# Two rows of wo per partition, loaded in 16 loads of 8 partitions on 8 of the 16 DMA engines

## Chip, cores, metric

One core of a Trainium2 chip. The metric is device time in microseconds (us), median over runs. A program on one core shows no second state here: all timed runs of both kernels count as fast.

## The reference, cut

```python
def _A_ref(x, k_cache, v_cache, wq, wo):        # B=2, Sq=1, D=512, H=32, Sk=8192, Dh=128, bf16
    q = (x @ wq).reshape(B, Sq, H, Dh).transpose(0, 2, 1, 3)
    scores = einsum("bhqd,bhkd->bhqk", q, k_cache) * (Dh ** -0.5)
    o = einsum("bhqk,bhkd->bhqd", softmax(scores), v_cache)
    return o.transpose(0, 2, 1, 3).reshape(B, Sq, H * Dh) @ wo
...
return x + _A_ref(layernorm(x), k_cache, v_cache, wq, wo) + relu_mlp(layernorm(x), w1, w2)
```

One token attends to 8192 cached positions. The two caches are 268 MB, so the kernel is a stream from memory with a short end: the last values, then `o @ wo`.

## The kernel before: the parts concerned

SP, the engine whose sequencer issues the loads, puts every large load on one queue (q1, 280.50 of the 280.66 MB). The matrix wo (4 MB, 32 rows of 1 KB on each of 128 partitions) comes last, in five chunks of rows, each with its own semaphore. PE, the matrix engine, waits for one chunk at a time and multiplies four times per row.

```python
wo_v = A_wo.rearrange("(p j) n -> p j n", j=WJ)          # WJ = 32 rows a partition
cuts = (0, 14, 21, 27, 30, WJ)
...
# SP
for i in range(2):                                        # the last V block, in two halves
    sl = slice(i * SLOT // 2, (i + 1) * SLOT // 2)
    sp.dma_start(vs[(NP - 1) % R][:, sl], V_all[(NP - 1) * P:NP * P, sl]).then_inc(dH[i], 16)
for c in range(NC):
    sl = slice(cuts[c], cuts[c + 1])
    sp.dma_start(wo_sb[:, sl, :], wo_v[:, sl, :]).then_inc(dW[c], 16)
sp.wait_ge(sE, 1)
sp.dma_start(out.rearrange("b s (c p) -> (b s c) p", p=P), osb[:]).then_inc(dO, 16)
...
# PE
for c in range(NC):
    pe.wait_ge(dW[c], 16)
    for j in range(cuts[c], cuts[c + 1]):
        for k in range(KT):                               # KT = 4
            t = pe.matmul(fin[:, k, :], lhsT=wo_sb[:, j, k * P:(k + 1) * P], rhs=OX[:, j, :],
                          start=False, stop=(j == WJ - 1 and k == KT - 1))
```

Of the kernel before, what the change touches and what calls it, by code (L numbers as in the profile page):

```python
# [19 lines left out]
def kernel(  # L20
# [13 lines left out]
    P = 128  # L34
# [3 lines left out]

    Bsz, Sq, D = A_x.shape
    _, H, Sk, Dh = A_k_cache.shape  # L40
    Dff = B_w1.shape[1]
    assert Dh == P and D % P == 0 and Dff % P == 0 and Sk % HP == 0
# [5 lines left out]
    WJ = H * Dh // P  # L48
# [18 lines left out]
    def sem(name):  # L67
        return tc.alloc_semaphore(name)
# [8 lines left out]
    wo_sb = w_sb[:, 0:WJ * D].rearrange("p (j n) -> p j n", j=WJ)  # L77
# [52 lines left out]
    dW = [sem(f"dWo{i}") for i in range(5)]  # L130
# [9 lines left out]
    K_all = A_k_cache.rearrange("b h (m kk) d -> (b h m) (kk d)", kk=KB)  # L140
    V_all = A_v_cache.rearrange("b h (m kk) d -> (b h m) (kk d)", kk=KB)
    wo_v = A_wo.rearrange("(p j) n -> p j n", j=WJ)
    cuts = (0, 14, 21, 27, 30, WJ)
    NC = len(cuts) - 1
    qp = ot[0][0:QG * Bsz, :]
    tpq = tp[1][:].rearrange("p g k -> p (g k)")[:, 0:N].rearrange(
# [10 lines left out]
    def load_k(t):  # L157
        nc.sync.dma_start(ks[t % R][:], K_all[t * P:(t + 1) * P, :]).then_inc(dK[t % R], 16)

    def load_v(t):  # L160
        nc.sync.dma_start(vs[t % R][:], V_all[t * P:(t + 1) * P, :]).then_inc(dV[t % R], 16)

    nc.sync.dma_start(vs[1][:], A_wq.rearrange("(p kt) n -> p (kt n)", kt=KT)).then_inc(dV[1], 16)  # L163
    nc.scalar.dma_start(xsb[:], A_x.flatten_outer_dims()).then_inc(dX, 16)
# [2 lines left out]
    @(lambda f: f(nc.sync))  # L167
    def _(sp):
        sp.dma_start(w1_sb, B_w1.rearrange("(p kt) f -> p kt f", kt=KT)).then_inc(dW1, 16)  # L169
        sp.dma_start(w2_sb, B_w2.rearrange("(p j) n -> p j n", j=FT)).then_inc(dW2, 16)  # L170
        load_k(0)
        load_k(1)
        load_v(0)
        for t in range(NP - 2):
            sp.wait_ge(pT[NG - 1], t + 1)
            load_k(t + R)
            sp.wait_ge(sW, t + 1)
            load_v(t + 1)
        sp.wait_ge(sW, NP - 1)
        for i in range(2):  # L180
            sl = slice(i * SLOT // 2, (i + 1) * SLOT // 2)
            sp.dma_start(  # L182
                vs[(NP - 1) % R][:, sl], V_all[(NP - 1) * P:NP * P, sl]
            ).then_inc(dH[i], 16)
        for c in range(NC):
            sl = slice(cuts[c], cuts[c + 1])
            sp.dma_start(wo_sb[:, sl, :], wo_v[:, sl, :]).then_inc(dW[c], 16)  # L187
        sp.wait_ge(sE, 1)
        sp.dma_start(
            out.rearrange("b s (c p) -> (b s c) p", p=P), osb[:]  # L190
        ).then_inc(dO, 16)
# [38 lines left out]
    def _(pe):  # L230
# [160 lines left out]

        pe.wait_ge(sV, 105)
        for c in range(NC):
            pe.wait_ge(dW[c], 16)
            for j in range(cuts[c], cuts[c + 1]):
                for k in range(KT):
                    t = pe.matmul(  # L397
                        fin[:, k, :],
                        lhsT=wo_sb[:, j, k * P:(k + 1) * P],
                        rhs=OX[:, j, :],  # L400
                        start=False,
                        stop=(j == WJ - 1 and k == KT - 1),
                    )
# [171 lines left out]
```

## Time and profile before

| | before |
|---|---|
| time, median of 3 | 660.91 us (660.84 to 661.13) |
| span in the profile | 658.6 us |
| DMA queue's share of 16 engines | 99.2% |
| last landing of wo | 654.85 us |
| last wo matmul's block begins | 654.90 us |

How to read it: the DMA engines are busy from end to end, so nothing but the edges of the stream can be gained. The last load's landing plus 3.8 us is the end of the span. The lines for this are shown in the prediction. A load's landing is the last of 16 semaphore increments, one from each DMA engine (chunk 4 of the kernel before: 128 packets of 2 KB, 16 writes of 4 bytes, 16 increments from 653.04 to 654.85); their single times are in the trace's records.

### The profile page before, as it was taken

Reading aid. Unit: us, or ns where it says so; the run is one execution under the profiler, and the core shown is the slowest. Engines: PE = TensorE matmul, PEld = TensorE weight load, DVE = VectorE, ACT = ScalarE, POOL = GpSimd, SP = SyncE. Lnnn points to the kernel's source line nnn. Section 1 sums busy time; section 2 is a strip of 40 time slices with the busy share of each in tenths; the row PEclk is TensorE's granted clock in tenths of the full one; section 3 lists DMA queues with packets and bytes.
Section 4 is the critical chain, followed back from the end, with each engine's and each line's share of the span. In section 5 each row is a group of like instructions: output and inputs, shape, how many; then the busy total and the mean of one; then the engine's idle time right before and its main releaser. Section 6 shows DMA issues by size and latency. Waiting matters only on the chain.

```text
span 658.6 us, 26859 instructions
## 1 busy us (share of the span) xinstructions
PE 559.9 (85%) x12737; PEld 535.1 (81%) x12737; DVE 253.2 (38%) x436; ACT 255.8 (39%) x403; POOL 9.0 (1%) x46
## 2 busy tenths in 40 slices
PE   2998799987989878879887887997878997887896
PEld 0488798987879878879887887987878987887895
DVE  1144344442434433334443343443434443333441
ACT  1043444443433434334353434344333444333340
POOL 1000000000000000000000000000000000000000
PEclk9799999998998988999898899898989998898988
DMA  8999999999999999999999999999999999999996
GB/s 365 430 444 418 439 430 429 432 428 442 422 442 424 436 428 432 432 428 444 420 442 428 432 430 430 434 430 442 424 436 428 432 432 428 440 424 442 426 424 281
DMA packets 10542, 280.66 MB, mean 426 GB/s; under 512 B 1186, under 2 KB 1188, under 8 KB 1700
## 3 DMA queue, kind: packets, MB, share of 16 engines
q1 hardware_dynamic: 10528, 280.50, 99.2%
q8 instruction: 9, 0.15, 0.1%
q14 instruction: 1, 0.01, 0.0%
q10 hardware_dynamic: 4, 0.00, 0.0%
HBM read 280.50 MB, written 0.00 MB: 426 GB/s over the span
## 4 chain that ended last, share of the span: by engine, by line
DMA 58%; PE 37%; ACT 2%; issue 1%; SPq 1%; ACTq 0%; DVE 0%
DMA ks<-in_A_k_cache_dram 54%; PE tp L285 21%; PE Sc L292 11%; PE ot L305 4%; DMA w_sb<-in_A_wo_dram 4%; ACT kT L412 2%; ACT L412 1%; SPq L187 0%; PE Sc L340 0%; SPq L182 0%; PE Sc L343 0%; SPq L170 0%; SPq L169 0%; SPq L163 0%; PE ot L397 0%
## 5 line engine op out<-in xcount | busy, mean ns | idle before, releaser
L285 PE MATMUL tp<-identb,ks 128*128 128x128 bf16 x4096 | 323.5, 229 | 68.4 <-DMA ks<-in_A_k_cache_dram 68.4
L412 DVE COPY kT<-tp 128x1024 bf16<-128x1024 bf16 x320 | 219.7, 691 | 324.3 <-PE tp L285 324.2
L285 PEld LDWEIGHTS tp<-identb,ks 128*128 128x128 bf16 x4096 | 254.8, 102 | 72.3 <-DMA ks<-in_A_k_cache_dram 72.2
L412 ACT COPY kT<-tp 128x1024 bf16<-128x1024 bf16 x192 | 194.3, 1012 | 233.4 <-PE tp L285 233.3
L292 PE MATMUL Sc<-q,kT 128*128 128x64 bf16 x4096 | 216.8, 196 | 7.6 <-ACT kT L412 5.7
L292 PEld LDWEIGHTS Sc<-q,kT 128*128 128x128 bf16 x4096 | 178.4, 100 | 11.3 <-ACT kT L412 9.0
L305 PE MATMUL ot<-prm,vs 128*128 128x64 bf16 x4224 | 156.1, 192 | 4.2 <-issue 4.2
L305 PEld LDWEIGHTS ot<-prm,vs 128*128 128x128 bf16 x4224 | 139.0, 97 | 7.0 <-issue 4.4
L525 ACT COPY nm<-Sc 128x2 f32<-128x2 f32 x32 | 5.1, 160 | 118.5 <-PE Sc L343 118.5
L529 ACT ACTIVATE prm<-Sc,nm 64x128 bf16<-64x128 f32 x64 | 25.7, 401 | 4.3
L466 DVE TENSOR_REDUCE mcol<-Sc 64x1 bf16<-64x128 f32 x64 | 18.6, 290 | 18.7 <-PE Sc L292 18.3
L412 ACT ACT_TABLE_LOAD x16 | 20.5, 1283 | 2.2
L240 PE MATMUL ot<-vs,xz 128*16 128x512 bf16 x32 | 9.5, 470 | 8.6 <-DMA vs<-in_A_wq_dram 8.6
L517 ACT COPY OTf<-ot 128x2 f32 x32 | 5.1, 160 | 26.9 <-PE ot L305 26.9
L471 DVE TENSOR_REDUCE mx<-Sc 1x2 bf16<-1x128 bf16 x32 | 8.9, 278 | 16.9 <-PE Sc L340 16.9
L240 PEld LDWEIGHTS ot<-vs,xz 128*16 128x16 bf16 x32 | 3.3, 105 | 14.4 <-issue 12.2
L225 POOL COPY q<-qb 128x2 bf16<-128x2 bf16 x32 | 5.8, 184 | 588.9 <-PE Sc L292 566.1
L529 ACT ACTIVATION_READ_ACCUMULATOR prm<-Sc,nm x64 | 11.8, 185 | 0.0
L442 DVE TENSOR_SCALAR qs<-ot 16x512 bf16<-16x512 f32 x1 | 0.7, 679 | 18.0 <-PE ot L240 18.0
L340 PE MATMUL Sc<-identb,mcol 128*1 128x128 bf16 x32 | 7.0, 217 | 0.0
L270 PE MATMUL Sc<-w_sb,hT 128*2 128x512 bf16 x14 | 5.8, 604 | 0.1
L343 PE MATMUL Sc<-mx,onesb 1*128 1x2 bf16 x32 | 5.5, 172 | 0.0
(56 smaller groups left out, 37.5 us busy)
## 6 DMA issues: line engine op xcount, KB each, us to landing
ks<-in_A_k_cache_dram SPq DMA_DIRECT2D x32, 4096.0 KB, 26.7
vs<-in_A_v_cache_dram SPq DMA_DIRECT2D x31, 4096.0 KB, 31.3
vs<-in_A_wq_dram SPq DMA_DIRECT2D x1, 4096.0 KB, 12.1
vs<-in_A_v_cache_dram SPq DMA_DIRECT2D x2, 2048.0 KB, 19.3
w_sb<-in_B_w_dram SPq DMA_DIRECT2D x2, 1792.0 KB, 17.9
w_sb<-in_A_wo_dram SPq DMA_DIRECT2D x1, 1792.0 KB, 25.4
w_sb<-in_A_wo_dram SPq DMA_DIRECT2D x1, 896.0 KB, 27.1
w_sb<-in_A_wo_dram SPq DMA_DIRECT2D x1, 768.0 KB, 28.5
```

The lines of the kernel that those rows point to most:

```text
L225: g.tensor_copy(q2[t % R][:], qb[:, 2 * t:2 * t + 2]).then_inc(sQ1, 1)
L240: i = pe.matmul(qp, lhsT=xz[:, kt, Z - g * Bsz:Z - g * Bsz + QG * Bsz], rhs=vs[1][:, (kt * QG + g) * 512:(kt * QG + g + 1) * 512], start=( ...
L270: i = pe.matmul(y, lhsT=hT[:, j, :], rhs=w2_sb[:, j, :], start=(j == 0), stop=(j == FT - 1),)
L285: t = pe.transpose(tp[e % 4][:, i, :], ks[r][:, kk * Dh:(kk + 1) * Dh], identb[:])
L292: t = pe.matmul(Sc[r][:, 2 * kk:2 * kk + 2 * REP], lhsT=kT[e % 4][:, i, :], rhs=rep(q2[r][:]), start=True, stop=True,)
L305: t = pe.matmul(ot[r][:, 0:2 * REP], lhsT=vs[r][:, kk * Dh:(kk + 1) * Dh], rhs=rep(prm[r][:, kk, :]), start=(kk == 0), stop=(kk == KB - 1),)
L340: pe.transpose(tr_of(r), mcol[r][:], identb[:]).then_inc(sT, 1)
L343: pe.matmul(bc_of(r), lhsT=onesb[:], rhs=mx[r][:], start=True, stop=True).then_inc(sB, 1)
L412: fn(kT[e % 4][:], tp[e % 4][:]).then_inc(kR[e], 1)
L466: m = v.tensor_reduce(out=mcol[i][half, :], in_=S_of(i)[half, :, u], axis=AX.X, op=ALU.max)
L471: v.tensor_reduce(out=mx[i][:], in_=tr_of(i).rearrange("o (u m) -> o u m", u=2), axis=AX.X, op=ALU.max, negate=True,).then_inc(sX, 1)
L529: x = a.activation(out=prm[i][half, :, u], in_=S_of(i)[half, :, u], func=ACTF.Exp, bias=nm[i][half, u:u + 1], scale=1.0, accum_out=RS[half ...
```

## The change

Its intent: not all 16 engines end together, so give more of the last bytes to some of them. Chunk 3 (now rows 28 and 29; row 27 moves to chunk 2) goes in 16 loads of 8 partitions. A load of 8 partitions has 8 late increments, one for each engine that carries it. The store of the output, also of 8 partitions, has one early and eight late in the kernel before (656.56, then 657.22 to 657.27). The same eight engines are taken to carry all sixteen loads. These eight are the "low" or "lowest" engines below, and an engine's number is its place in the order in which the engines join the loads of experiment 1.

```diff
-    cuts = (0, 14, 21, 27, 30, WJ)
+    cuts = (0, 14, 21, 28, 30, WJ)
+    LOW = 3
...
+    def load_wo(sp, c):
+        step = 8 if c == LOW else P
+        for p in range(0, P, step):
+            sl = slice(p, p + step), slice(cuts[c], cuts[c + 1])
+            sp.dma_start(wo_sb[sl], wo_v[sl]).then_inc(dW[c], 16)
...
-            sl = slice(cuts[c], cuts[c + 1])
-            sp.dma_start(wo_sb[:, sl, :], wo_v[:, sl, :]).then_inc(dW[c], 16)
+            load_wo(sp, c)
...
-            pe.wait_ge(dW[c], 16)
+            pe.wait_ge(dW[c], 16 * (P // 8) if c == LOW else 16)
```

## The prediction

> **What bounds the kernel now.** I read the page first, then the chain of waits from 620 us on, the timeline of the last eight microseconds, and the DMA issues.
>
> The page, slices and queues:
>
> ```profile
> DMA  8999999999999999999999999999999999999996
> GB/s 365 430 444 418 439 430 429 432 428 442 422 442 424 436 428 432 432 428 444 420 442 428 432 430 430 434 430 442 424 436 428 432 432 428 440 424 442 426 424 281
> q1 hardware_dynamic: 10528, 280.50, 99.2%
> q8 instruction: 9, 0.15, 0.1%
> ```
>
> The reader is to see that the 16 DMA engines are busy 99.2% of the span. The kernel streams 280.5 MB at about 430 GB/s and no engine sets the time while that goes on. Only the edges can be shortened: the last of the 40 slices falls to 281 GB/s. The second thing is the small line: nine instruction fetches (16 KB each, 0.15 MB) share those engines.
>
> The chain of waits after 620 us (start, duration, what):
>
> ```profile
> 625.26 0.43 SPq L187
> 625.69 0.04 issue
> 625.73 29.12 DMA w_sb<-in_A_wo_dram
> 654.85 0.05 issue
> 654.90 0.39 PE ot L397 x8
> 655.29 0.02 issue
> 655.31 0.18 DVE yT L502
> 655.49 0.04 issue
> 655.53 0.28 PE tp L406
> 655.81 0.02 issue
> 655.84 0.21 DVE osb L504
> ```
>
> The end is set by the last load of wo (issued 29 us earlier, landed at 654.85), then 8 matmuls, two copies, a transpose and the store. From 654.85 to the end of the span at 658.6 is 3.8 us that this change doesn't touch.
>
> The timeline of the wo matmuls (start, duration, what, idle before and its releaser):
>
> ```profile
> 650.17 2.23 PE L397 MATMUL ot<-OX,w_sb 128*128 128x2 bf16 x83 [0.32 <-DVE OX L498]
> ...
> 653.34 1.40 PE L397 MATMUL ot<-OX,w_sb 128*128 128x2 bf16 x36 [0.25 <-DMA w_sb<-in_A_wo_dram]
> 654.90 0.37 PE L397 MATMUL ot<-OX,w_sb 128*128 128x2 bf16 x8 [0.16 <-DMA w_sb<-in_A_wo_dram]
> ```
>
> The first two chunks (21 rows of wo, 84 matmuls) are done at 652.4 at 2.23/83 = 27 ns a matmul; then PE waits for each chunk. So PE has about 0.9 us of slack just before chunk 2 and almost none behind it.
>
> No view splits a load by engine, but the trace records each increment of a load's semaphore. Sorted, the 16 increments of the last four loads (own reading of these records, us) are:
>
> ```
> chunk 1 (rows 14-20): 649.55 to 649.98 nine engines, 651.24 to 651.40 seven
> chunk 2 (rows 21-26): 651.47 to 651.86 eight,        653.10 to 653.29 eight
> chunk 3 (rows 27-29): 652.38 to 652.82 eight,        654.04 to 654.21 eight
> chunk 4 (rows 30-31): 653.04 to 653.44 eight,        654.67 to 654.85 eight
> ```
>
> So half of the engines end 1.4 us before the other half. The first three loads of the kernel show no such split (spread 0.38 us). It grows one engine at a time, in step with the instruction fetches: seven fetches between 29.6 and 107.2 us, seven late engines from 108 us on, and an eighth fetch at 650.36 after which chunk 2 has eight late. Each fetch puts its engine back by some 1.3 us, and as the queues never run dry the delay stays to the end. The early half idles for its last 1.4 us while the late half sets the end.
>
> [...]
>
> **The change, part by part.** Row 27 of each partition moves from chunk 3 into chunk 2, which has 7 rows; chunk 3 has rows 28 and 29, in 16 loads; chunk 4 is unchanged. PE's instructions are the same and in the same order; only one wait's number differs.
>
> Issue. SP needs 0.43 + 0.05 us a load (chain). Sixteen take 7.7 us, so chunk 4 is issued at about 633 rather than 625.7. It is needed at 653: hidden, with 20 us to spare.
>
> Transfer. Packet durations in the trace: 2048 B 84 ns, 3072 B 121, 6144 B 234, 7168 B 272, semaphore write 9. An engine carries 8 packets of a 128-partition load. Before, chunks 2 to 4: 8 x (234 + 121 + 84) + 27 = 3.54 us on every engine. After, on a high engine: 8 x (272 + 84) + 18 = 2.87 us, that is 0.67 less. On a low engine: 8 x 272 + 9, then 16 x (84 + 9), then 8 x 84 + 9, together 4.36 us, that is 0.82 more. If the low engines are the early ones, they end at 653.04 to 653.44 plus 0.82 = 653.9 to 654.3, and the late ones at 654.67 to 654.85 less 0.67 = 654.0 to 654.2. The two halves would be level, and the last landing about 654.3 instead of 654.85: 0.55 us earlier. That two rows level it so exactly makes me think that the change was sized for this skew.
>
> PE. Chunk 2 lands 8 x 38 ns = 0.3 us later, at about 653.6, and behind it stand 44 matmuls as before. At 27 to 30 ns (24 weight loads in 0.72 us) they take 1.2 to 1.3 us and end at about 654.9, against 655.29 before. So PE takes back some of the 0.55 us, and the net is -0.35 to -0.4 us: the new order of limits is chunk 2's landing, then PE without a pause. 660.91 - 0.35 = 660.55.
>
> **The rivals.**
> (a) The early engines are not the low ones. Which eight carried fetches can't be told from this trace. For low = early: the skew is eight to eight at the end and the change fits it. Against: nothing labels the engines. If the low ones were late, they would end at 654.85 + 0.82 = 655.7 and the time would be about 661.7. If the groups are mixed, one late low engine is enough for the same. I give this 12%.
> (b) [...] It would give a last landing of 654.8 to 655.1 and 660.9 to 661.2. 20%.
> (c) One semaphore write behind every 2 KB packet. In the trace it costs 9 ns but stands behind eight packets at least. [...] 10%.
> (d) The ninth fetch began at 654.27 on an engine that was idle then, since no landing was put back by it. If it now starts while that engine still has chunk 4 to bring, one landing moves back by 1.3 us, to 655.5, and the time to 661.5. [...] I give it 8%.
> The remaining 50% is the main path.
>
> **Range and chances.** The main path gives 660.55, (b) 661.0, (a) and (d) about 661.6, (c) 662.4; the middle of this mixture lies between the first two, at 660.75. The three runs of before spread by 0.3 us. Range 660.1 to 662.1. Two per cent is 13.2 us, and the largest of the rivals, (c), moves the time by 1.5. Within 2% therefore 98.5%.
>
> **What the profile will show.** Right: instruction fetches at the same places; 16 issues of 16 KB for wo; chunk 4's landings in one cluster of at most 0.6 us that ends near 654.3; PE's last 44 matmuls nearly without a pause from 653.6. Wrong: chunk 4's landings still in two groups with the late one at or after 654.8 (a, b or d; an early group not moved and a late one moved back says a, both halves late says b); chunk 3's 256th increment over 1.9 us after chunk 2's early ones (c); a stream that differs before 648 us would mean that something outside of my account changed.

The main path's sum came to 660.55 us. Of (b), that the choice of partitions takes the gain back, only the outcome stands, 660.9 to 661.2 (661.0 in the mixture) with 20%; (c) had 0.14 us more for each of the 16 small loads, 2.2 us in all, which makes 662.4, with 10%. The 0.14 was the author's estimate and isn't in the trace: of chunk 2 the last 6 KB packet ends at 652.81 us and the load lands at 653.29. With these two and with (a) and (d) the mixture's middle came to 660.75.

## The result and the profile after

Before 660.92 us (660.84 to 661.13, six runs), after 663.75 us (663.53 to 663.92, six runs). The ratio is 1.0042, 95% interval 1.0029 to 1.0055. A ratio here is the mean time of one kernel's fast runs over that of the other's of the same rounds, so not quite the ratio of the medians quoted. It is 2.8 us slower and clear of the spread, where 0.2 us faster was the centre of the prediction.

The page's queue line and the chain of waits of the changed kernel (start, duration, what):

```profile
q1 hardware_dynamic: 10640, 280.50, 98.9%
```

```profile
635.59 22.11 DMA w_sb<-in_A_wo_dram
657.70 0.05 issue
657.75 0.60 PE ot L404 x16
658.35 0.02 issue
658.37 0.18 DVE yT L509
```

The bytes are the same, in 112 more packets. The chain has the form it had before: wo's load, matmuls, copies. But the landing that PE waits for is at 657.70 and no longer at 654.85, 2.85 us later. It is chunk 3's (the chain's 16 matmuls are those of chunks 3 and 4 together). The span grew by 3.1 us, from 658.6 to 661.7; the other 0.2 us is that 16 matmuls and no longer 8 stand behind this landing (0.60 us instead of 0.39).

The timeline of the wo matmuls after:

```profile
650.32 2.23 PE L404 MATMUL ot<-OX,w_sb 128*128 128x2 bf16 x83 [0.32 <-DVE OX L505]
...
654.70 0.91 PE L404 MATMUL ot<-OX,w_sb 128*128 128x2 bf16 x28 [1.54 <-DMA w_sb<-in_A_wo_dram]
657.75 0.58 PE L404 MATMUL ot<-OX,w_sb 128*128 128x2 bf16 x16 [2.14 <-DMA w_sb<-in_A_wo_dram]
```

Against the lines of before: PE now stands idle 1.5 us ahead of chunk 2 and 2.1 us ahead of chunk 3. It isn't PE that takes the gain back, as the prediction had it; there is no gain on the DMA side to take.

Sixteen issues at SP, from the same chain further up:

```profile
626.09 0.29 SPq L169
...
629.51 1.17 SPq L169
...
633.16 1.78 SPq L169
634.93 0.04 issue
634.98 0.57 SPq L169
```

A small load takes 0.29 us to issue, and the later ones are held up to 1.8 us. Chunk 4 is issued at about 635, still 16 us before its data move, so this costs nothing.

The increments by time (own reading of the trace's records, us):

```
before  chunk 2  651.47-651.86 eight           653.10-653.29 eight
        chunk 3  652.38-652.82 eight           654.04-654.21 eight
        chunk 4  653.04-653.44 eight           654.67-654.85 eight
after   chunk 2  651.71-652.50 seven, 653.28, 653.84, 654.26-654.65 seven
        chunk 3  128 increments from 652.00 on; the last: 656.86 656.88 657.07 657.08 657.27 657.29 657.48 657.50 657.68 657.70
        chunk 4  653.00-655.99 thirteen, 656.89, 657.89, 657.91
```

Three things are to be seen. Chunk 2 lands 1.4 us later than before on the late engines, where 0.3 was predicted. Chunk 3 ends with two engines counting alone, one increment each every 0.2 us. And the two that do so begin at about 657.7 - 16 x 0.2 = 654.5, which is when the late engines have just landed chunk 2: these are low engines, and they are late ones.

From that I formed three parts of a theory. **S**: a small load costs each of its engines 0.2 us, whatever is in it. **L**: some of the lowest 8 engines are late. **C**: the small loads slow the other engines' packets, depending on which partitions they load. The rival to S is **B**, that cost goes with bytes; the rival to L is the prediction's assumption; the rival to C is that any work added to low engines slows the rest.

### The profile page after: what moved, and what is told of

Read it like the earlier page. It is cut to its first block, busy times and chain, and to the rows that moved or that the text cites. A ratio compares the mean times of both kernels' runs of the same rounds, so it can differ in the third digit from the quotient of the medians.

```text
span 661.7 us, 26874 instructions
## 1 busy us (share of the span) xinstructions
PE 561.3 (85%) x12737; PEld 536.2 (81%) x12737; DVE 253.1 (38%) x436; ACT 255.9 (39%) x403; POOL 8.9 (1%) x46
## 4 chain that ended last, share of the span: by engine, by line
DMA 54%; PE 39%; ACT 2%; SPq 2%; issue 1%; DVE 0%; ACTq 0%
DMA ks<-in_A_k_cache_dram 49%; PE tp L292 21%; PE Sc L299 11%; PE ot L312 4%; DMA w_sb<-in_A_wo_dram 3%; DMA vs<-in_A_wq_dram 2%; ACT kT L419 2%; SPq L169 2%; PE ot L247 1%; PE Sc L277 1%; ACT L419 1%; PE ot L260 1%; PE Sc L347 0%; SPq L190 0%; PE Sc L350 0%
## 5 line engine op out<-in xcount | busy, mean ns | idle before, releaser
L404 PE MATMUL ot<-OX,w_sb 128*128 128x2 bf16 x128 | 3.9, 165 | 4.4 <-DMA w_sb<-in_A_wo_dram 3.7
L404 PEld LDWEIGHTS ot<-OX,w_sb 128*128 128x128 bf16 x128 | 3.6, 99 | 4.8 <-DMA w_sb<-in_A_wo_dram 3.9
```

## The experiments

Unless said otherwise three rounds and results correct. The kernel before gave 660.76, 660.92, 660.96 and 660.99 us. The numbers follow the argument and not the time: experiments 2 and 13 ran after 1 and 3 to 9, and before 10 to 12. Single executions of experiments 3, 7, 12 and 13 lie 1.1 to 1.6 us above the median of their kernel without a lower clock; they count as fast, and I don't know why.

### 1. Which engines are late

```diff
         for c in range(NC):
+            if c == 1:
+                for m in range(16):
+                    sp.dma_start(prb[0:m + 1, m, :], wo_v[0:m + 1, m, 0:16]).then_inc(dP[m], 16)
             sl = slice(cuts[c], cuts[c + 1])
```

> The kernel before, with 16 tiny loads (1, 2, ... 16 partitions of 32 bytes, each on its own semaphore) queued between chunk 0 and chunk 1 of wo. A load of m partitions is carried by m engines, so the increments of the loads of m and m-1 partitions differ by engine m-1, and whether it lands in the early or the late group says if that engine is late. The load on 16 partitions should show 7 late increments, as chunk 1 did before. If the prediction's assumption holds, the loads of 1 to 8 partitions have no late increment at all. If its rival (a) holds, some of them have: I now expect 2 or 3 late among the lowest 8, since in the changed kernel two to three engines still count up the third chunk alone at the end. Time 661 to 662.5; the tiny loads themselves are not the subject.

662.62 us (one run, state unknown). Increments of the tiny loads, us:

```
4 partitions   647.58 647.74 647.77 648.28
5 partitions   647.76 647.93 647.94 648.35 648.46
6 partitions   647.94 648.10 648.12 648.54 648.63 649.23
7 partitions   648.12 648.26 648.28 648.72 648.80 649.08 649.43
8 partitions   647.68 648.30 648.45 648.46 648.91 648.99 649.29 649.64
16 partitions  647.82 648.33 649.12 649.40 649.62 649.69 649.82 649.83 649.93 649.95 650.08 650.14 650.46 650.50 650.92 651.47
```

Each engine's increment follows its own of the load before by 0.17 to 0.20 us; what is left over is the new engine, and the engines are numbered in the order in which they join. Engines 0 to 3, 7, 8, 11 and 15 come first by 647.4 to 647.9 and are early; engine 4 comes at 648.35, some 0.6 us behind; engines 5, 6, 9, 10, 12, 13 and 14 come at 649.07 to 649.50. That makes seven late, as chunk 0's own increments in this run have it (647.25 to 648.16 nine, 648.89 to 649.33 seven). Two of the lowest 8 are late and one is in between: L holds. The loads are of 32 bytes a partition and still take 0.17 to 0.20 us each, which is S at its purest: bytes can't be the cost. The records of these packets last 9 ns, so in nearly all of the step no byte of the load is seen to move.

The probe isn't quite neutral. A fetch of 8 KB at 630.4 us (311 ns), which the kernel before does not have, falls between a load in which one landing is 0.45 us behind the first and the next, in which it is 0.88. The changed kernel has such a fetch too (631.7 us); so engine 4 is in between in these kernels, and not in the kernel before.

### 2. The same in the changed kernel

The same 16 loads inserted in the changed kernel, between chunks 0 and 1.

> The changed kernel with the 16 tiny loads (1 to 16 partitions) between chunks 0 and 1, to read off which engines are late in it. Expected as in the kernel before: engines 5 and 6 late among the lowest 8, others of the late ones above 8; which means that the lowest 8 are not the early half. Each tiny load again costs every engine that carries it 0.18 to 0.20 us although it has 32 bytes. The time is 2 to 3 us above the changed kernel's and is not the subject.

665.30 us (one run, state unknown). The new increments of the loads of 5 to 8 partitions are 648.33, 649.30, 649.20 and 647.78: engine 4 in between, 5 and 6 late, 7 early, as in experiment 1. The fetches are at nearly the same places as without the probe (29.6 to 107.3 us, then 650.8). So the eight lowest engines are not the early half in either kernel, as far as a probe can tell; experiments 11 and 12 show without one that engines 4 to 7 are not all early.

### 3. The cuts alone

```diff
-    cuts = (0, 14, 21, 27, 30, WJ)
+    cuts = (0, 14, 21, 28, 30, WJ)
```

> Only the cuts are moved (chunk 2 has rows 21 to 27, chunk 3 rows 28 and 29), every load spans 128 partitions and 16 engines. Every theory: the same bytes on every engine as before, last landing as before at about 654.85 us, chunk 2 at about 653.6, time 660.9 within 0.4. If it is slower by more than 1 us, the cuts and not the 16 loads cost the time.

660.98 us against 660.76, ratio 1.0008 (0.9991 to 1.0025). The chain:

```profile
625.89 29.11 DMA w_sb<-in_A_wo_dram
655.00 0.05 issue
```

Last landing 655.00, chunk 2 at 653.72, and 7 KB packets took 276 ns. The cuts are innocent; everything is in the 16 loads.

### 4. The 16 loads with partitions 4 apart

```diff
+        for p in range(0, P, 32):
+            for r in range(4):
+                pp = slice(p + r, p + 32, 4)
+                sp.dma_start(wo_sb[pp, sl, :], wo_v[pp, sl, :]).then_inc(dW[c], 16)
```

> As the changed kernel, but each of the 16 loads takes 8 partitions that lie 4 apart[...]. [...] Semaphore theory (each small load costs an engine 0.2 us[...]): 16 times 0.2 us as before, time 663.5 to 664.

The "semaphore theory" is S, and its name is not a cause that was shown. A rival in which the choice of partitions sets it had 0.1 us a load and about 661.5 us.

663.43 us against 660.76, ratio 1.0040 (1.0024 to 1.0057).

```profile
636.45 20.75 DMA w_sb<-in_A_wo_dram
657.20 0.05 issue
```

Chunk 3's last landing is 657.20: still 0.21 us an increment on two engines to the very end. Neighbouring partitions don't make the small load's 0.2 us; S stands. The choice of partitions has a share elsewhere: the 7 KB packets of chunk 2 that began between 651.9 and 654.5 took 435 ns in the changed kernel, 385 here and 276 with the cuts alone. But chunk 2's last landing, 654.58, is hardly earlier than the changed kernel's 654.65, so for small loads most of this slowing is not explained by neighbouring partitions. What makes the rest of it was not shown.

### 5. Eight loads of 16 partitions

```diff
-        step = 8 if c == LOW else P
+        step = 16 if c == LOW else P
```

> Chunk 3 in 8 loads of 16 partitions: every one of the 16 engines carries 8 of them, each of 2 KB with a semaphore write behind it. No engine gets more bytes than before. Semaphore theory: 8 times 0.2 us instead of 8 x 84 ns + 9 = 0.68, so every engine ends 0.9 us later, last landing near 655.8, time near 661.8. Theory that only the uneven placement costs (more work for engines that are late): 660.9 as before. [...]

The same rival had between 661 and 662 us.

662.25 us against 660.76, ratio 1.0020 (1.0004 to 1.0037); chunk 3 landed at 656.25 and chunk 4 at 656.47, where with the cuts alone chunk 4 landed at 655.00. Now no engine has more bytes than another (199 packets under 512 bytes from 648 to 660 us against 87 with the cuts alone: 8 x 16 writes in place of 16), and it still costs 1.3 us of time against the cuts alone; 0.9 was expected from S. The rest agrees with slower 7 KB packets (393 ns) and chunk 2 at 654.53, 0.8 later than with the cuts alone.

### 6 and 7. Half and twice the bytes in the same 16 loads

```diff
-    cuts = (0, 14, 21, 28, 30, WJ)
+    cuts = (0, 14, 21, 29, 30, WJ)          # one row; with 26 instead of 29: four rows
```

> As the changed kernel, but the 16 loads carry one row (1 KB a packet, half the bytes) and chunk 2 carries eight rows. Theory S (each small load costs its engine a fixed 0.2 us[...], whatever its size): 16 x 0.2 us as before, and the longer chunk 2 adds 8 x 37 ns = 0.3 us: last landing about 658.0, time about 664.0. Theory B (the cost goes with the bytes, 0.1 us a KB): 1.6 us less in the loads, 0.3 more in chunk 2: about 662.4.

> As the changed kernel, but the 16 loads carry four rows (4 KB a packet, twice the bytes) and chunk 2 carries five rows. Theory S: 4 KB take 0.16 us, still under the fixed 0.2, so the loads take as long as with 2 KB and the shorter chunk 2 saves 8 x 75 ns = 0.6 us: last landing about 657.1, time about 663.2. Theory B: 16 x 0.4 = 6.4 us in place of 3.2, less 0.6: about 666.3.

The 0.16 us for 4 KB is an estimate, from 84 ns for 2 KB in the kernel before.

One row: 663.55 us, ratio 1.0034 (1.0015 to 1.0053). Four rows: 664.37 us, ratio 1.0049 (1.0026 to 1.0072). Chunk 3's last increments:

```
1 KB packets   ... 656.66 656.70 656.87 656.90 657.08 657.11 657.28 657.31 657.52
4 KB packets   ... 657.21 657.27 657.43 657.49 657.66 657.70 657.87 657.90 658.08 658.28
```

Both come in steps of 0.20 to 0.24 us an engine. Four times the bytes, the same step: S, and B falls (it had 662.4 and 666.3). My sums missed by 0.5 and 1.2 us because chunk 2 moved otherwise than its rows say: its last landing was 654.34 with eight rows and 654.59 with five. The bigger the small loads' packets, the slower chunk 2's packets beside them: from 651.9 to 654.5 they took 1.2 times their shortest time beside packets of 1 KB (375 against 309 ns), 1.6 times beside 2 KB (435 against 272) and 1.7 times beside 4 KB (338 against 196). That is C, which I had left out of those sums.

### 8 and 9. Spare bytes: sixteen loads against two

The kernel with the cuts alone, and in addition 256 KB of wo loaded again into a buffer that nobody reads, ahead of chunk 3, on the lowest 8 engines.

```diff
+            if c == 3:
+                for p in range(0, P, 8):        # two large loads: for p in (0, 8), rows 0:16
+                    sp.dma_start(junk[p:p + 8, 0:2], wo_v[p:p + 8, 0:2]).then_inc(dJ, 16)
```

> The kernel before with the moved cuts and its 128-partition loads, and in addition 256 KB of wo loaded a second time into a buffer that nothing reads: 16 loads of 8 partitions x 2 KB, ahead of chunk 3, on the lowest 8 engines. Theory S: the late low engines get 16 x 0.2 = 3.2 us more than in the kernel with the cuts alone (last landing 655.0): 658.2, time about 664.1. If only bytes counted: 16 x 93 ns = 1.5 us more, time about 662.4.

> The same spare 256 KB on the same 8 engines in 2 loads of 8 partitions x 16 KB. Theory S: two packets and two semaphore writes an engine, 2 x (0.6 + 0.01) = 1.2 us more than with the cuts alone: last landing 656.2, time about 662.1, so 2 us less than with 16 loads of the same bytes. [...] If only bytes counted: no difference to the 16 loads.

The rival in which the choice of partitions counts, by an estimate that no run had shown, came to 4.8 us, 665 us or more.

Sixteen loads: 664.24 us, ratio 1.0047 (1.0028 to 1.0066), as S has it (664.1). That it fits so well is partly luck: chunk 2 landed 1.1 us late here too (654.79), and chunks 3 and 4 landed only 0.2 and 0.6 us behind the spare loads where the sum had 1.36. Two loads: 664.69 us, ratio 1.0051 (1.0031 to 1.0070), where S alone had 662.1. The timeline of the wo matmuls with two large loads:

```profile
656.46 0.91 PE L403 MATMUL ot<-OX,w_sb 128*128 128x2 bf16 x28 [2.94 <-DMA w_sb<-in_A_wo_dram]
658.96 0.37 PE L403 MATMUL ot<-OX,w_sb 128*128 128x2 bf16 x8 [1.59 <-DMA w_sb<-in_A_wo_dram]
659.59 0.37 PE L403 MATMUL ot<-OX,w_sb 128*128 128x2 bf16 x8 [0.26 <-DMA w_sb<-in_A_wo_dram]
```

Chunk 2, which has nothing to do with the spare loads, lands 2.7 us later than with the cuts alone (656.41 against 653.72; the profiled execution took 665.41 us, the longest of the four). The 16 KB packets that began between 651.9 and 654.5 took 1.8 us in the middle, and chunk 2's 7 KB ones beside them 794 ns instead of 276. So S isn't all, and C is large when packets are. The rival, with 665, was nearer than S with 662.1.

### 10. The two large loads with partitions 4 apart

```diff
-                for p in (0, 8):
-                    sp.dma_start(junk[p:p + 8, 0:16], wo_v[p:p + 8, 0:16]).then_inc(dJ, 16)
+                for pp in (slice(0, 32, 4), slice(1, 32, 4)):
+                    sp.dma_start(junk[pp, 0:16], wo_v[pp, 0:16]).then_inc(dJ, 16)
```

> The spare 256 KB on the lowest 8 engines in 2 loads of 8 partitions x 16 KB again, but the partitions lie 4 apart[...]. Conflict theory (neighbouring partitions [...] made 16 KB take 1.8 us and slowed the other engines to a third in the run before): now about 0.61 us a 16 KB packet, 7 KB packets of the others back at 275 ns, 1.2 us more than with the cuts alone on the late low engines: last landing 656.2, time about 662.1. If work added to the lowest 8 engines slows the rest wherever it goes: 664.7 again.

661.89 us against 660.99, ratio 1.0013 (0.9997 to 1.0030).

```profile
653.89 0.91 PE L403 MATMUL ot<-OX,w_sb 128*128 128x2 bf16 x28 [0.69 <-DMA w_sb<-in_A_wo_dram]
655.40 0.37 PE L403 MATMUL ot<-OX,w_sb 128*128 128x2 bf16 x8 [0.61 <-DMA w_sb<-in_A_wo_dram]
656.04 0.38 PE L403 MATMUL ot<-OX,w_sb 128*128 128x2 bf16 x8 [0.26 <-DMA w_sb<-in_A_wo_dram]
```

Nothing but the choice of partitions was changed, and 2.8 us are gone. The 16 KB packets took 616 ns and the others' 7 KB ones 275, as without any spare load, and the last landing is 655.99 (656.2 expected). So the slowing depends here on which partitions are loaded, and the same added work on partitions that lie apart slowed nobody. One rival stays untested: the rows of wo that are read move together with the partitions (`wo_v[pp]`), so this run doesn't tell the writing side from the reading side. Nor is the slowing confined to the 16 KB packets of the spare loads: in experiment 9 all 7 KB packets of the seven or eight engines that still had some took 0.45 to 1.1 us. Why neighbouring partitions do this was not shown.

### 11 and 12. Eight small loads on 4 engines, and on 8

Spare loads as before, 2 KB packets, 4 apart, eight of them; on engines 0 to 3, which are early, or on 0 to 7.

```diff
+                for pp in [slice(b + r, b + r + 16, 4) for b in (0, 32) for r in range(4)]:   # or b + r + 32
+                    sp.dma_start(junk[pp, 0:2], wo_v[pp, 0:2]).then_inc(dJ, 16)
```

> The kernel before with the moved cuts and 8 spare loads of 4 partitions x 2 KB (4 apart) ahead of chunk 3: engines 0 to 3 alone, which the tiny loads showed early. 8 x 0.2 = 1.6 us added to engines that end at 653.0 to 653.5: 654.6 to 655.1, no later than the late engines' 655.0. Time as with the cuts alone, 661.0, at most 0.3 above.

> The same with 8 spare loads of 8 partitions x 2 KB (4 apart): engines 0 to 7. If engines 5 and 6 are late here as the tiny loads showed, they end 1.6 us later: last landing 656.6, time about 662.6. If the prediction's assumption holds (the lowest 8 are early), no difference to the 8 loads of 4 partitions: 661.0 to 661.3.

Four engines: 660.91 us, ratio 0.9998 (0.9981 to 1.0015). Eight: 662.00 us, ratio 1.0021 (1.0004 to 1.0037). The timelines of the wo matmuls, first with 4 engines, then with 8:

```profile
653.84 1.62 PE L403 MATMUL ot<-OX,w_sb 128*128 128x2 bf16 x44 [1.28 <-DMA w_sb<-in_A_wo_dram]
```

```profile
653.86 0.91 PE L403 MATMUL ot<-OX,w_sb 128*128 128x2 bf16 x28 [1.30 <-DMA w_sb<-in_A_wo_dram]
655.46 0.76 PE L403 MATMUL ot<-OX,w_sb 128*128 128x2 bf16 x16 [0.69 <-DMA w_sb<-in_A_wo_dram]
```

Chunk 2 is on time in both. On early engines the eight small loads are free: they are landed at 653.59 and PE runs through without another pause. With engines 4 to 7 in it they land at 655.21, two engines alone at the end, and PE waits for chunk 3 behind them. L is shown. The expectation for eight engines was 0.6 too high: I had added chunks 3 and 4 (1.36 us) behind the small loads, but they landed 0.2 and 0.6 us after them. That would fit if the next packets were on their way while the small loads' increments were still being counted; it was not shown.

### 13. An attempt at a version that wins

Chunk 1 with eight rows: partitions 16 to 127 in one load, partitions 0 to 15 in 4 loads of 4 partitions on engines 0 to 3. Chunk 2 shrinks to five rows.

```diff
+            lo = 16 if c == LOW else 0
+            sp.dma_start(wo_sb[lo:P, sl, :], wo_v[lo:P, sl, :]).then_inc(dW[c], 16)
+            for p in range(0, lo, 4):
+                sp.dma_start(wo_sb[p:p + 4, sl, :], wo_v[p:p + 4, sl, :]).then_inc(dW[c], 16)
```

> An attempt to beat both kernels. The tiny loads of the first run showed engines 0 to 3 early, and 5 and 6 among the late ones. Chunk 1 has rows 14 to 21: partitions 16 to 127 in one load over 16 engines (7 packets of 8 KB each), partitions 0 to 15 in 4 loads of 4 partitions, which engines 0 to 3 carry alone, 4 packets of 8 KB each, above the 0.2 us that a small load costs. Chunk 2 shrinks to five rows. Engines 4 to 15: 8 x 37 ns = 0.3 us less than before; engines 0 to 3: 4 x 0.31 - 0.3 = 0.94 us more, ending at 654.4 instead of 653.4, if they are early in this kernel too. Then the last landing moves from 654.85 to 654.55 and the time from 660.8 to 660.5, a difference hardly above the spread of the runs. If one of the lowest four engines is late here: 655.8 and 661.7.

The 7 packets an engine are an estimate, 112 packets over the 16 engines that a load of 128 partitions uses in the kernel before.

663.82 us against 660.96 in five rounds, ratio 1.0050 (1.0036 to 1.0064): it fails by 3 us. Chunk 1's 8 KB packets took 575 ns on the mean after 651.9 instead of the 310 assumed. Why was not shown: the load of 112 partitions and the 4 small loads, each of four neighbouring partitions, were not tried apart, and experiments 9 and 10 only make the neighbouring partitions a likely cause. I found no version that beats the kernel before.

## Why the prediction was wrong, point by point

- **The bound** (the stream's end, last landing plus 3.8 us): right but for 0.2 us. It became 4.0, with 16 matmuls behind the landing.
- **The skew by instruction fetches** (half of the engines 1.4 us late, one by one): right, and seen in every run. The "1.3 us" for one fetch is the gap between the groups; the landing that the first fetch put back moved by some 1.5 us (32.73 in the kernel before, with the other fifteen from 31.01 to 31.39; the fetch began at 29.57 and took 1.06).
- **Issue is hidden**: right, though later loads were held up to 1.8 us.
- **"If the low engines are the early ones"**: this step failed. The prediction took it for the main path since two rows would level the halves so exactly, which is no evidence. Engines 5 and 6 are late and 4 is behind. Rival (a) named it with 12%. In the changed kernel it makes two engines start on the 16 loads at about 654.5 rather than 652.0. In experiments 11 and 12 the same choice is worth 1.1 us.
- **"16 x (84 + 9)"** for a low engine's small loads: this term was mis-sized. It measured 16 x 0.2 = 3.2 us instead of 1.49. Rival (c) had 0.23 us a load and gave it 10%. Whether it is the semaphore write or another cost of each load can't be told: every load in these runs has a semaphore. By my estimate this step alone was enough to lose: a low engine that starts early, at 652.0, is through with chunks 3 and 4 at 652.0 + 3.2 + 0.2 = 655.4. Sorted into series 0.2 us apart, chunk 3's increments show that the five early ones of the low engines were through with it only at 655.2 to 655.8. The prediction had the low engines through with chunk 4 as well by 653.9 to 654.3, and the kernel before ended at 654.85.
- **"Chunk 2 lands 0.3 us later"**: it landed 1.36 later (654.65). About 0.4 is the cuts (653.72 in experiment 3); the other 0.9 goes with slower packets of chunk 2 beside the small loads (435 ns for 7 KB). For small loads, partitions 4 apart brought these 435 ns to 385 and not to the 276 of the cuts alone (experiment 4); what slows them beyond that was not shown. Rival (b) was only a cap on the gain.
- **"PE takes back some"**: didn't come to pass; PE waited.
- **Rival (d)**, the ninth fetch: it had no share that is seen. It began at 654.59 us and took 1.11, but the two engines that end last count on in steps of 0.2 us without a gap.

The sum closes: chunk 2 on the late engines at 654.26 to 654.65 (up to 0.9 of it by slower packets), 16 x 0.2 = 3.2 us, and chunk 4 0.2 behind, is 657.7 to 658.1; measured 657.91. The prediction treated the rivals as alternatives and spread the chances over them, with the worst at 662.4. They hold together and add: late engines, slow loads, slowed packets. That is why the time fell outside the range.

How much of the 2.8 us each part is worth by itself can't be split cleanly, because part of an early engine's slow loads is hidden. From the runs: eight small loads on early engines free (experiment 11); on late ones 0.14 us apiece in the end (1.1 us over eight, experiments 12 and 11); neighbouring partitions 0.5 us of chunk 3's landing for 2 KB packets (657.70 against 657.20, experiment 4) and 2.8 us of time for 16 KB ones (experiments 9 and 10).

## What to carry to other kernels

Before moving work to "idle" DMA engines, find out which engines are idle: tiny loads of 1, 2, 3, ... partitions read it off in one run, and here the number of late engines follows the instruction fetches (seven fetches from 29.6 to 107.2 us and seven late engines after, eight after the one at 650.36). Count loads per engine as well as bytes: a queued load costs each engine it runs on 0.2 us here (0.17 to 0.20 with packets of 32 bytes, 0.20 to 0.24 with 1 and 4 KB), so below some 5 KB a partition the number of loads decides (an estimate from 84 ns for 2 KB; 4 KB was the most tried). Here loads of few partitions and large packets did better with partitions that lie apart (616 ns against 1.8 us for 16 KB, 661.89 us against 664.69). And when several rivals to a prediction act on different terms of one sum, add them before setting the range.
